# Pair slots for weight parts, and two weight slots lent as staging buffers, in a window-attention and two-MoE-layer kernel

## The chip, the cores and the metric

The kernel runs on one core of one Trainium2 chip. The metric is the device time of one execution in microseconds (us), lower is better. A core has five engines that run side by side, each taking its own instructions in order: TensorE (PE, matmuls), VectorE (DVE), ScalarE (ACT), GpSimd (POOL) and SyncE (SP, used here to issue DMA transfers). They wait for each other by semaphores. PE writes its results into PSUM banks; everything else lies in SBUF.

## The reference

All inputs are float32. Attention with a window of 64 keys over 4 batches, 8 heads, 576 positions and 64 columns a head; then x of 2304 tokens by 512 columns goes through two layers:

```python
scores = scale * np.matmul(q, k.transpose(0, 1, 3, 2))       # window of 64 keys, softmax
x = np.matmul(attn, v)                                       # -> 2304 x 512

h = x @ w_in                                                 # first layer, d_ff 2048
g = np.where(pos, h, np.where(neg, 0.0, (h + beta) ** 2 / (4.0 * beta)))
x = g @ w_out

h = x @ w_in2                                                # second layer, d_ff 1024
solu = h * softmax(h)
ln = (solu - mu) / np.sqrt(var + 1e-06) * g_ln
out = ln @ w_out2
```

## The kernel before

**Numbers in two parts.** A float32 matrix product is made of three products of a faster format: each operand is split into hi and lo, and hi x hi, hi x lo and lo x hi are added. For the first layer the split weights stay in SBUF: for each of 16 ranges f of 128 hidden columns there are `wih{f}`, `wil{f}` (of w_in) and `woh{f}`, `wol{f}` (of w_out), each in a slot of its own in pool `w_p`, named by its tag.

**How a weight comes in.** A *unit* is 128 x 512 float32-pairs of w_in or w_out, 512 KiB. There are 32, in the order w_in range 0, w_out range 0, w_in range 1 and so on; unit n is range n // 2, counted from 0, so "the 15th unit" is unit 14. `w1_unit` picks the slots, `w_unit` takes a staging buffer `st` (tag "st", `NST` = 5 buffers in a ring) and issues the transfer: units 0 to 4 on SP, the others on POOL. Then come three steps, one for each call of `w_conv`: `split_a` (ACT, L132), `split_b` (two DVE instructions, L136 and L137), and `split_c` (ACT writes the hi part, L145; DVE subtracts and writes the lo part, L146). After the L146 of its unit a staging buffer is free. POOL takes its instructions in order too, so a transfer that waits for its buffer holds back all those behind it.

**The stage.** Tokens are worked in six blocks j of 384. For a block and each range f, `moe_h` makes 12 matmuls into `ps_h` (L496, needing wih and wil of f), ACT and DVE turn that into gh and gl (L505, L506, L511, L512, L515), and `moe_y` adds 12 matmuls into four accumulators `acc` (L526, needing woh and wol). Block 0 needs every range's weights for the first time, so it runs along with their arrival; this is the stage that the change touches. The other blocks find all weights in place. After the last block come the products of the second layer (L712) and its output (L827).

**Attention in between.** The blocks' inputs are made between the matmuls: for group g (192 tokens, two heads) PE makes scores `ps_s` (L352), DVE adds the mask and finds the extremum (L360), ACT takes the exponentials (L366), DVE sums and scales (L377 to L386), PE transposes p into `ps_p` (L400, L402), ACT copies that to pT (L405, L407), PE multiplies by v into `ps_x` (L421), and ACT and DVE split the result into xh (L428) and xl (L429). Groups 0 to 7 make block 0's input, 8 to 15 block 1's. Groups 0 to 17 go one by one, later ones in pairs (L442, L476). One group's keys and queries lie in `kq`, in one of two buffers by turns.

**What sets the order.** The program is written as one sequence of such steps, and a scheduler orders each engine's instructions by its own model of when their inputs are there. That includes its model of when a weight transfer lands. On the chip the order of every engine is then fixed.

**Slots lent before.** Queries and keys of the first tokens lie in the slots of ranges 12 to 15 of w_in until those are loaded; the second layer's weights, its sums `xs` and `u` and its split activations later use the slots of both kinds.

Of the kernel before, what the change touches and what calls it, by code (L numbers as in the profile page):

```python
# [20 lines left out]
def kernel(  # L21
# [28 lines left out]
    NG = NTILES * NP  # L50
    NST = 5
    G0, F0, NC, NQ, NV = 6, 2, 4, 6, 7
# [67 lines left out]

    def w_unit(src, hi, lo, gain=None, eng=nc.sync):
        st = stage["p"].tile([128, 512, 2], U32, tag="st", bufs=NST, name="wst")
        if src.shape[0] == 128 and len(src.shape) == 3:
            w_dma = eng.dma_start(out=st.rearrange("p (k f) t -> p k (f t)", k=src.shape[1]), in_=src)  # L124
        else:
            w_dma = eng.dma_start(out=st.rearrange("p f t -> p (f t)"), in_=src)  # L126
        wdma.append(w_dma.ins)
        return st, hi, lo, gain
# [32 lines left out]

    def wtile(tag):
        return w_p.tile([128, 512], F32R, tag=tag, name=tag)

    def w1_unit(f, which):
        if which == 0:
            hi, lo = wtile(f"wih{f}"), wtile(f"wil{f}")
            wih[f] = hi.rearrange("p (k f) -> p k f", k=KC)
            wil[f] = lo.rearrange("p (k f) -> p k f", k=KC)
            src = w_in[:, f * 256:(f + 1) * 256].rearrange("(k p) f -> p k f", p=128)  # L170
        else:
            hi, lo = woh[f], wol[f] = wtile(f"woh{f}"), wtile(f"wol{f}")
            src = w_out[f * 128:(f + 1) * 128, :]
        return w_unit(src, hi, lo, None, nc.sync if len(wdma) < NST else nc.gpsimd)

# [42 lines left out]
    def w2_load(n):  # L218
        hi, lo = w2oh[n], w2ol[n] = wtile(f"woh{n}"), wtile(f"wol{n}")
        for t, z in enumerate((hi, lo)):  # L220
            nc.sync.dma_start(out=as_f32(z), in_=w2d[8 + n][:, t * 512:(t + 1) * 512])
# [23 lines left out]
    def w2_split(n):  # L245
        v_ = w2v.pop(WORDER[n])
        hi, lo = w2h[WORDER[n]], w2l[WORDER[n]] = wtile(f"wih{n}"), wtile(f"wil{n}")
        nc.scalar.copy(hi, v_)
# [12 lines left out]
    def load_qk(g):  # L261
# [3 lines left out]
        if g < NPE:  # L265
            for src, dst, tag, r0, n in (
                (q, qn, "wih", tl * TT, TT // 2),
                (k, kn, "wil", tl * TT - back, (TT + back) // 2),
            ):
                for r in range(2):  # L270
                    if t < 2:
                        a = w_p.tile([128, 512], F32, tag=f"{tag}{14 - 2 * t + r}", name="qkn")
                    else:
                        a = at_p.tile([128, 512], F32, tag="qk", bufs=5, name="qkn")
                    dst[t, r] = a[0:n, :]
            for h0, h1 in ((0, 2), (2, H)) if t == 0 else ((0, H),):
# [391 lines left out]
    def x2_prep(p):  # L668
        r = x2r.pop(p)
        a11, a12, a21, a22 = (r[:, 2 * k:2 * k + 2, 128 * t:128 * t + 128] for t in range(2) for k in range(2))  # L670
        s = [
            (w_p.tile([128, 512], F32, tag=f"{y}{14 + p % 2}", name="xs") if p else
             d_p.tile([128, 512], F32, tag="o", name="xs")).rearrange("p (z k n) -> p z k n", z=2, k=2)
            for y in ("wih", "wil")
        ]
        s1, s2, s3, s4 = (s[z // 2][:, z % 2] for z in range(4))
# [41 lines left out]
    u = {}  # L718
    PARTS = (("P1", "P6", "P7", "P5", "P4"), ("P2", "P3"))

    def st_p(m, y):
# [5 lines left out]
        elif y == "P1":  # L727
            for z in range(4):
                tag = f"{'woh' if z < 2 else 'wol'}{12 + 2 * (z % 2) + p % 2}"
                u[z + 1] = w_p.tile([128, 512], F32, tag=tag, name="u")  # L730
        if y == PARTS[m % 2][0]:
# [69 lines left out]
    def st_t2(m):  # L801
        lnh[m], lnl[m] = {}, {}
        l_ = ln.pop(m)
        for a in range(2):
            hi, lo = wtile(f"woh{8 + 2 * (m % 2) + a}"), wtile(f"wol{8 + 2 * (m % 2) + a}")
            lnh[m][a], lnl[m][a] = (z.rearrange("p (k t) -> p k t", t=128) for z in (hi, lo))
# [188 lines left out]
```

## Time and profile before

| | us |
|---|---|
| median of 3 runs | 706.09 (705.32 to 706.83) |
| profiled execution | 703.17 |
| its span, first to last instruction | 701.4 |
| PE busy in the span | 678.1 (97%) |
| DVE busy | 448.3 (64%) |
| ACT busy | 412.5 (59%) |
| POOL busy | 134.2 (19%) |

The profile is of one execution. Times are counted from the span's start. A row of the time line gives start, length, engine, line, operation and tiles, and in square brackets how long the engine had been idle before it and what ended that. Matmuls overlap, and their ends are modelled: two neighbouring ones are listed with 0.33 us each and start 0.17 us apart. PE is busy nearly everywhere from about 135 us on; its idle time lies in front of that, while weights, attention and the first block go on together.

### The profile page before, as it was taken

Reading aid. Unit: us, or ns where it says so; the run is one execution under the profiler, and the core shown is the slowest. Engines: PE = TensorE matmul, PEld = TensorE weight load, DVE = VectorE, ACT = ScalarE, POOL = GpSimd, SP = SyncE. Lnnn points to the kernel's source line nnn. Section 1 sums busy time; section 2 is a strip of 40 time slices with the busy share of each in tenths; the row PEclk is TensorE's granted clock in tenths of the full one; section 3 lists DMA queues with packets and bytes.
Section 4 is the critical chain, followed back from the end, with each engine's and each line's share of the span. In section 5 each row is a group of like instructions: output and inputs, shape, how many; then the busy total and the mean of one; then the engine's idle time right before and its main releaser. Section 6 shows DMA issues by size and latency. Waiting matters only on the chain.

```text
span 701.4 us, 12574 instructions
## 1 busy us (share of the span) xinstructions
PE 678.1 (97%) x4439; PEld 625.6 (89%) x4439; DVE 448.3 (64%) x1213; ACT 412.5 (59%) x1006; POOL 134.2 (19%) x178
## 2 busy tenths in 40 slices
PE   6899888899999999999999999999999999999998
PEld 5689788799999999999999999999997888888887
DVE  4789889646445555454455552643289999999850
ACT  5889777665656655665566565364455555445451
POOL 1112221100001000021112111662272322220000
PEclk9999999999999999999999999999999999999999
DMA  9996896625353523346351211562024455444331
GB/s 194 253 241 161 218 245 196 148 35 108 72 116 112 116 64 76 77 129 126 85 113 61 106 41 51 173 202 93 1 83 142 155 178 189 158 147 150 103 109 46
DMA packets 150551, 88.94 MB, mean 127 GB/s; under 512 B 118616, under 2 KB 134744, under 8 KB 150488
## 3 DMA queue, kind: packets, MB, share of 16 engines
q1 hardware_dynamic: 135160, 49.84, 30.2%
q0 software_dynamic: 12592, 33.57, 14.9%
q10 hardware_dynamic: 2736, 4.72, 1.8%
q8 instruction: 35, 0.57, 0.3%
q14 instruction: 28, 0.23, 0.1%
HBM read 63.97 MB, written 24.12 MB: 126 GB/s over the span
## 4 chain that ended last, share of the span: by engine, by line
PE 71%; issue 13%; POOL 4%; DVE 4%; DMA 3%; SPq 3%; ACT 2%; POOLq 0%; DVEq 0%
PE acc L526 21%; PE ps_h L496 21%; PE ps_o L827 14%; PE P L712 9%; DMA wst<-in_moe_w_in_dram 3%; POOL wil L249 2%; PE ps_x L476 2%; PE ps_s L442 2%; PE ps_p L402 2%; SPq L279 1%; DVE gl L515 1%; POOL wst L124 1%; SPq L302 1%; POOL wst L126 1%; DVE x2p L692 1%
## 5 line engine op out<-in xcount | busy, mean ns | idle before, releaser
L511 DVE SCALAR_TENSOR_TENSOR u<-u,ps_h 128x384 f32<-128x384 f32 (+1 forms) x98 | 53.3, 544 | 142.3 <-ACT u L506 141.4
L496 PE MATMUL ps_h<-xh,wih 128*128 128x384 f32 (+1 forms) x392 | 132.0, 337 | 3.1 <-ACT wih L145 3.0
L526 PE MATMUL acc<-gl,woh 128*128 128x384 f32 (+1 forms) x392 | 130.3, 334 | 2.1 <-DVE gl L515 2.1
L496 PE MATMUL ps_h<-xl,wih 128*128 128x384 f32 (+1 forms) x392 | 130.7, 334 | 0.4 <-DVE xl L429 0.4
L496 PE MATMUL ps_h<-xh,wil 128*128 128x384 f32 (+1 forms) x392 | 130.9, 334 | 0.0
L526 PE MATMUL acc<-gh,wol 128*128 128x384 f32 (+1 forms) x392 | 129.3, 332 | 0.0
L526 PE MATMUL acc<-gh,woh 128*128 128x384 f32 (+1 forms) x392 | 123.8, 341 | 2.3 <-ACT gh L512 2.3
L505 ACT ACTIVATE u<-ps_h,half 128x384 f32<-128x384 f32 (+1 forms) x98 | 56.1, 574 | 97.5 <-PE ps_h L496 97.3
L515 DVE TENSOR_TENSOR gl<-u,gh 128x384 fp32r<-128x384 f32 (+1 forms) x98 | 62.6, 640 | 35.2 <-ACT gh L512 34.6
L512 ACT CAST gh<-u 128x384 fp32r<-128x384 f32 (+1 forms) x98 | 49.7, 508 | 49.9 <-DVE u L511 34.8
L496 PEld LDWEIGHTS ps_h<-xh,wih 128*128 128x128 f32 x392 | 74.1, 189 | 4.5 <-ACT wih L145 3.6
L526 PEld LDWEIGHTS acc<-gh,woh 128*128 128x128 f32 x392 | 72.0, 188 | 6.2 <-ACT gh L512 3.5
L526 PEld LDWEIGHTS acc<-gl,woh 128*128 128x128 f32 x392 | 73.7, 188 | 3.1 <-DVE gl L515 2.7
L496 PEld LDWEIGHTS ps_h<-xl,wih 128*128 128x128 f32 x392 | 74.1, 189 | 1.0 <-DVE xl L429 0.8
L496 PEld LDWEIGHTS ps_h<-xh,wil 128*128 128x128 f32 x392 | 74.1, 189 | 0.1
L526 PEld LDWEIGHTS acc<-gh,wol 128*128 128x128 f32 x392 | 73.6, 188 | 0.1
L712 PE MATMUL P<-wih,x2p 128*128 128x512 f32 x216 | 71.6, 390 | 0.7 <-DVE x2p L692 0.7
L827 PE MATMUL ps_o<-woh,wol 128*128 128x512 f32 (+1 forms) x152 | 57.6, 379 | 0.0
L827 PE MATMUL ps_o<-woh,woh 128*128 128x512 f32 (+1 forms) x152 | 57.5, 379 | 0.0
L827 PE MATMUL ps_o<-wol,woh 128*128 128x512 f32 (+1 forms) x152 | 57.5, 378 | 0.0
L506 ACT ACTIVATE u<-u 128x384 f32<-128x384 f32 (+1 forms) x98 | 51.1, 522 | 1.9
L712 PEld LDWEIGHTS P<-wih,x2p 128*128 128x128 f32 x216 | 40.4, 188 | 9.2 <-DVE x2p L692 1.1
(123 smaller groups left out, 1191.8 us busy)
## 6 DMA issues: line engine op xcount, KB each, us to landing
wst<-in_moe_w_out_dram POOLq DMA_DIRECT2D x22, 512.0 KB, 7.4
wst<-in_moe_w_in_dram POOLq DMA_DIRECT2D x21, 512.0 KB, 5.5
vw<-in_v_dram SPq DMA_DIRECT2D x32, 256.0 KB, 5.3
lnd<-e SPq DMA_DIRECT2D x16, 512.0 KB, 2.7
lT<-lnd SPq DMA_DIRECT2D x64, 128.0 KB, 3.0
x2d<-xo POOLq DMA_DIRECT2D x24, 192.0 KB, 2.6
out_dram<-o ACTq DMA_DIRECT2D x17, 256.0 KB, 2.0
w2d<-w2st POOLq DMA_DIRECT2D x8, 512.0 KB, 3.0
```

Source lines behind the costliest of these rows:

```text
L249: nc.gpsimd.tensor_tensor(lo, v_, as_f32(hi), op=ALU.subtract)
L402: nc.tensor.transpose(ps[:, i * 128:i * 128 + 128], p[:, i, :], ident)
L442: nc.tensor.matmul(ps[x][64 * c:64 * c + 64, i * 128 + c0:i * 128 + 128], z[r, KQ + i * 64:KQ + i * 64 + 64], z[r, i * 64 + c0:i * 64 + 12 ...
L496: nc.tensor.matmul(ps, a, bb[:, kc, c], start=(n == 0), stop=(n == 3 * KC - 1))
L505: nc.scalar.activation(u, ps, ACTF.Relu, bias=half, scale=0.5)
L506: nc.scalar.activation(u, u, ACTF.Square)
L511: g = nc.vector.scalar_tensor_tensor(u, u, 1.0, ps, op0=ALU.min, op1=ALU.max)
L512: return nc.scalar.copy(hi, u).ins, g.ins
L515: nc.vector.tensor_tensor(lo, u, as_f32(hi), op=ALU.subtract)
L526: nc.tensor.matmul(acc[j, e][:, c], a, bb, start=(f == 0 and n == 0 and c.start == 0), stop=(f == NF - 1 and n == 2),)
L712: nc.tensor.matmul(ps, l, r, start=(n == 0), stop=(n == 5))
L827: nc.tensor.matmul(ps, a[kk // 4][:, kk % 4, :], b[kk][:, c:c + w], start=(n == 0), stop=(n == 3 * NK2 - 1),)
```

## The change

1. The hi and lo part of a weight share one slot of 128 x 2 x 512 (`wi{f}`, `wo{f}`), and all that uses these slots later takes them in pairs.
2. `NX` = 2: from unit 14 on, and up to unit 27, two of each seven units take the slot `wo15` or `wo14` as staging buffer instead of one of the ring's five: units 14 and 21 take wo15, 15 and 22 take wo14. The final contents of these slots are units 31 and 29.
3. Each unit's transfer from unit 6 on is kept behind the one before it in the scheduler's order.

```diff
-    NST = 5
+    NST, NX = 5, 2
...
-    def w_unit(src, hi, lo, gain=None, eng=nc.sync):
-        st = stage["p"].tile([128, 512, 2], U32, tag="st", bufs=NST, name="wst")
+    def w_unit(src, hi, lo, gain=None, eng=nc.sync, slot=None):
+        if slot is None:
+            st = stage["p"].tile([128, 512, 2], U32, tag="st", bufs=NST, name="wst")
+        else:
+            st = w_p.tile([128, 512, 2], U32, tag=slot, name="wst")
...
-    def wtile(tag):
-        return w_p.tile([128, 512], F32R, tag=tag, name=tag)
+    def wpair(tag, dt=F32R):
+        return w_p.tile([128, 2, 512], dt, tag=tag, name=tag)
+
+    def wtiles(tag):
+        t = wpair(tag)
+        return t[:, 0, :], t[:, 1, :]
...
-            hi, lo = wtile(f"wih{f}"), wtile(f"wil{f}")
+            hi, lo = wtiles(f"wi{f}")
...
-            hi, lo = woh[f], wol[f] = wtile(f"woh{f}"), wtile(f"wol{f}")
+            hi, lo = woh[f], wol[f] = wtiles(f"wo{f}")
             src = w_out[f * 128:(f + 1) * 128, :]
-        return w_unit(src, hi, lo, None, nc.sync if len(wdma) < NST else nc.gpsimd)
+        n = len(wdma)
+        x = NX - 1 - (n - 14) % (NST + NX) if n >= 14 else -1
+        slot = f"wo{NF - NX + x}" if x >= 0 and n < 2 * (NF - NX) else None
+        with ExitStack() as order:
+            if n > NST:
+                order.enter_context(tc.issue_after(wdma[-1]))
+            return w_unit(src, hi, lo, None, nc.sync if n < NST else nc.gpsimd, slot)
...
     def x2_prep(p):
...
-        s = [
-            (w_p.tile([128, 512], F32, tag=f"{y}{14 + p % 2}", name="xs") if p else
-             d_p.tile([128, 512], F32, tag="o", name="xs")).rearrange("p (z k n) -> p z k n", z=2, k=2)
-            for y in ("wih", "wil")
-        ]
+        if p:
+            s = wpair(f"wi{14 + p % 2}", F32)
+            s = s[:, 0, :], s[:, 1, :]
+        else:
+            s = [d_p.tile([128, 512], F32, tag="o", name="xs") for _ in range(2)]
+        s = [z.rearrange("p (z k n) -> p z k n", z=2, k=2) for z in s]
...
-            for z in range(4):
-                tag = f"{'woh' if z < 2 else 'wol'}{12 + 2 * (z % 2) + p % 2}"
-                u[z + 1] = w_p.tile([128, 512], F32, tag=tag, name="u")
+            for z in range(2):
+                t = wpair(f"wo{12 + 2 * z + p % 2}", F32)
+                u[z + 1], u[z + 3] = t[:, 0, :], t[:, 1, :]
```

The uses in `w2_load`, `w2_split`, `load_qk` and `st_t2` change in the same way, from two tags to one pair. The order that comes of it differs from about unit 14 to the end of block 0; what follows stands nearly as before.

POOL, the weight transfers of units 13 to 18, with what each waits for: DMASW is the landing of an earlier transfer into the same buffer, DVE the last step of its split. Before:

```order
L126 DMA wst<-in_moe_w_out_dram 128x1024 [waits DMASW3_49,DVE_49]
L124 DMA wst<-in_moe_w_in_dram 128x4x256 [waits DMASW4_49,DVE_49]
L126 DMA wst<-in_moe_w_out_dram 128x1024 [waits DMASW5_49,DVE_49]
L124 DMA wst<-in_moe_w_in_dram 128x4x256 [waits DMASW6_49,DVE_49]
L126 DMA wst<-in_moe_w_out_dram 128x1024 [waits DMASW7_49,DVE_49]
L124 DMA wst<-in_moe_w_in_dram 128x4x256 [waits DMASW0_49,DVE_49]
```

Of the change, the same place:

```order
L129 DMA wst<-in_moe_w_out_dram 128x1024 [waits DMASW3_49,DVE_49]
L127 DMA wst<-in_moe_w_in_dram 128x4x256
L129 DMA wst<-in_moe_w_out_dram 128x1024
L127 DMA wst<-in_moe_w_in_dram 128x4x256 [waits DMASW4_49,DVE_49]
L129 DMA wst<-in_moe_w_out_dram 128x1024 [waits DMASW5_49,DVE_49]
L127 DMA wst<-in_moe_w_in_dram 128x4x256 [waits DMASW6_49,DVE_49]
```

Units 14 and 15 wait for nothing any more, and unit 16 has the wait that unit 14 had.

DVE around the last step of the last split (`wol_1409`, in the change `wo_1373`): p<-p,rs is the scaling of a group's softmax, ISA its first step. Before:

```order
L382 TENSOR_TENSOR p<-p,rs 128x64
L386 TENSOR_TENSOR p<-p,rs 128x256
L146 TENSOR_TENSOR wil_1335<-wst,wih_1334 128x512
L511 SCALAR_TENSOR_TENSOR u<-u,ps_h 128x384
L146 TENSOR_TENSOR wol_1409<-wst,woh_1408 128x512
L515 TENSOR_TENSOR gl<-u,gh 128x384
L360 ISA p,mx<-ps_s,mask 128x64
```

Of the change:

```order
L149 TENSOR_TENSOR wo_1373<-wst,wo_1373 128x512
L392 TENSOR_TENSOR p<-p,rs 128x64
L396 TENSOR_TENSOR p<-p,rs 128x256
L525 TENSOR_TENSOR gl<-u,gh 128x384
L521 SCALAR_TENSOR_TENSOR u<-u,ps_h 128x384
L525 TENSOR_TENSOR gl<-u,gh 128x384
L370 ISA p,mx<-ps_s,mask 128x64
```

The scaling of a group that stood ahead of the last split stands behind it; the ISA that follows is group 15's before and group 14's in the change.

PE at the end of the stage, from the last acc matmuls to the first ones of block 1 (`ps_h`): kq_125 holds groups with odd numbers, kq_124 those with even ones; three instructions make one group's scores or transposes. Before:

```order
L526 MATMUL acc_754<-gl,woh_1408 128x384
L526 MATMUL acc_754<-gh,wol_1409 128x384
L352 MATMUL ps_s<-kq_124 128x128 x3
L421 MATMUL ps_x<-pT,vw 64x64 x6
L402 MATMUL ps_p<-ident,p 128x128 x3
L352 MATMUL ps_s<-kq_125 128x128 x3
L496 MATMUL ps_h<-xh,wih_146 128x384
```

Of the change:

```order
L536 MATMUL acc_735<-gh,wo_1373 128x384
L362 MATMUL ps_s<-kq_125 128x64
L362 MATMUL ps_s<-kq_125 128x128 x2
L431 MATMUL ps_x<-pT,vw 64x64 x6
L410 MATMUL ps_p<-ident,p 64x128
L362 MATMUL ps_s<-kq_124 128x128 x3
L412 MATMUL ps_p<-ident,p 128x128 x2
L431 MATMUL ps_x<-pT,vw 64x64 x6
L412 MATMUL ps_p<-ident,p 128x128 x3
L362 MATMUL ps_s<-kq_125 128x128 x3
L506 MATMUL ps_h<-xh,wi_144 128x384
```

Group 15's scores, ps_x of group 14 and the transposes of group 15 stand ahead of the last acc matmuls before, and behind them in the change.

## Rows read from the trace of the kernel before

**Rows 1.** Stretches: length, busy of PE, PEld, DVE, ACT, POOL, granted clock, DMA share, GB/s.
```profile
57.00:67.20 10.20, 10.20 (x72) 9.81 (x71) 10.14 (x31) 9.22 (x24) 1.42 (x3) 1.00 0.65 171
67.20:121.50 54.30, 48.25 (x310) 44.42 (x309) 48.09 (x131) 41.59 (x99) 11.50 (x18) 1.00 0.89 223
...
129.40:134.32 4.92, 2.57 (x29) 2.18 (x28) 2.95 (x13) 2.32 (x9) 2.12 (x4) 1.00 0.75 182
134.32:701.00 566.68, 561.54 (x3609) 519.56 (x3608) 342.23 (x867) 311.18 (x718) 111.28 (x135) 1.00 0.38 108
```

**Rows 2.** Waits of PE after 134.32 us: us in total, times, longest.
```profile
PE acc L526 <- DVE gl L515: 1.3, 1, 1.3
PE P L712 <- DVE x2p L692: 0.7, 1, 0.7
```

**Rows 3.** Waits of PE in 67.20 to 121.50 us.
```profile
PE ps_h L496 <- ACT wih L145: 3.0, 2, 1.6
PE acc L526 <- ACT gh L512: 2.3, 4, 1.3
PE acc L526 <- DVE gl L515: 0.8, 1, 0.8
```

**Rows 4.** Waits of ACT and of DVE in 67.20 to 121.50 us, the longest.
```profile
ACT wst L132 <- DMA wst<-in_moe_w_in_dram: 7.6, 6, 2.1
...
DVE wst L136 <- DMA wst<-in_moe_w_in_dram: 4.1, 5, 1.2
```

**Rows 5.** Time line of POOL: the issues of units 14, 15, 16, 18 and 31.
```profile
57.84 0.77 POOL L124 DMA_DIRECT2D wst<-in_moe_w_in_dram  x1 [2.13 <-DVE gl L515]
64.20 0.54 POOL L126 DMA_DIRECT2D wst<-in_moe_w_out_dram  x1 [5.60 <-DVE xl L429]
67.09 0.76 POOL L124 DMA_DIRECT2D wst<-in_moe_w_in_dram  x1 [2.35 <-DVE wol L146]
...
73.54 0.76 POOL L124 DMA_DIRECT2D wst<-in_moe_w_in_dram  x1 [5.15 <-DVE wst L137]
...
110.02 0.54 POOL L126 DMA_DIRECT2D wst<-in_moe_w_out_dram  x1 [0.87 <-DVE wil L146]
```

**Rows 6.** The staging tiles wst in 57.00 to 121.50 us: from issue to landing.
```profile
DMA to landing us min/median/max: 4.1/5.3/7.8
```

**Rows 7.** Time line of PE at the end of the stage.
```profile
129.40 0.83 PE L352 MATMUL ps_s<-kq 128*128 128x128 f32 x6
130.16 0.71 PE L421 MATMUL ps_x<-pT,vw 64*64 64x64 f32 x12
133.23 0.52 PE L402 MATMUL ps_p<-ident,p 128*128 128x128 f32 x3 [2.35 <-DVE p L386]
133.58 0.83 PE L352 MATMUL ps_s<-kq 128*128 128x128 f32 x6
134.32 0.44 PE L496 MATMUL ps_h<-xh,wih 128*128 128x384 f32 x1
```

**Rows 8.** Time line of PE around one wait for a weight.
```profile
78.04 0.86 PE L526 MATMUL acc<-gh,woh 128*128 128x384 f32 x4
80.24 0.44 PE L496 MATMUL ps_h<-xh,wih 128*128 128x384 f32 x1 [1.34 <-ACT wih L145]
80.52 0.34 PE L496 MATMUL ps_h<-xl,wih 128*128 128x384 f32 x1
```

**Rows 9.** Time line of ACT: group 15's copies of pT.
```profile
127.51 0.26 ACT L405 COPY pT<-ps_p 64x128 f32<-64x128 f32 x1
127.68 0.36 ACT L407 COPY pT<-ps_p 128x256 f32<-128x256 f32 x1
```

**Rows 10.** Stretches early in the program, columns as in rows 1.
```profile
22.70:26.13 3.43, 3.36 (x38) 3.06 (x38) 1.97 (x14) 2.71 (x13) 0.00 (x0) 1.00 1.07 383
29.54:32.95 3.41, 1.87 (x21) 1.29 (x20) 2.86 (x8) 3.41 (x12) 0.00 (x0) 1.00 1.10 166
32.95:36.36 3.41, 3.41 (x25) 2.97 (x24) 2.54 (x10) 3.38 (x10) 0.54 (x1) 0.50 0.61 98
```

More of the change, by code (lines that the diff above doesn't have):

```diff
@@ L218, in w2_load @@
     def w2_load(n):
-        hi, lo = w2oh[n], w2ol[n] = wtile(f"woh{n}"), wtile(f"wol{n}")
+        hi, lo = w2oh[n], w2ol[n] = wtiles(f"wo{n}")
         for t, z in enumerate((hi, lo)):
@@ L246, in w2_split @@
         v_ = w2v.pop(WORDER[n])
-        hi, lo = w2h[WORDER[n]], w2l[WORDER[n]] = wtile(f"wih{n}"), wtile(f"wil{n}")
+        hi, lo = w2h[WORDER[n]], w2l[WORDER[n]] = wtiles(f"wi{n}")
         nc.scalar.copy(hi, v_)
@@ L265, in load_qk @@
         if g < NPE:
[L266 to L275, printed above, removed]
+            for r in range(2):
+                if t < 2:
+                    a = wpair(f"wi{14 - 2 * t + r}", F32)
+                    a = a[:, 0, :], a[:, 1, :]
+                else:
+                    a = [at_p.tile([128, 512], F32, tag="qk", bufs=5, name="qkn") for _ in range(2)]
+                qn[t, r], kn[t, r] = a[0][0:TT // 2], a[1][0:(TT + back) // 2]
             for h0, h1 in ((0, 2), (2, H)) if t == 0 else ((0, H),):
@@ L670, in x2_prep @@
         a11, a12, a21, a22 = (r[:, 2 * k:2 * k + 2, 128 * t:128 * t + 128] for t in range(2) for k in range(2))
-        s = [
-            (w_p.tile([128, 512], F32, tag=f"{y}{14 + p % 2}", name="xs") if p else
-             d_p.tile([128, 512], F32, tag="o", name="xs")).rearrange("p (z k n) -> p z k n", z=2, k=2)
-            for y in ("wih", "wil")
-        ]
+        if p:
+            s = wpair(f"wi{14 + p % 2}", F32)
+            s = s[:, 0, :], s[:, 1, :]
+        else:
+            s = [d_p.tile([128, 512], F32, tag="o", name="xs") for _ in range(2)]
+        s = [z.rearrange("p (z k n) -> p z k n", z=2, k=2) for z in s]
         s1, s2, s3, s4 = (s[z // 2][:, z % 2] for z in range(4))
@@ L804, in st_t2 @@
         for a in range(2):
-            hi, lo = wtile(f"woh{8 + 2 * (m % 2) + a}"), wtile(f"wol{8 + 2 * (m % 2) + a}")
+            hi, lo = wtiles(f"wo{8 + 2 * (m % 2) + a}")
             lnh[m][a], lnl[m][a] = (z.rearrange("p (k t) -> p k t", t=128) for z in (hi, lo))
```

## The prediction

> **What bounds the kernel now.** I read the table of stretches first. From 134.32 us to the end TensorE (PE) is busy 561.54 of 566.68 us, and PE's list of waits for that part has only 1.3 and 0.7 us [rows 1, 2]; it runs at PE's pace, so what PE gains or loses before 134.32 reaches the end nearly whole. In 57.00 to 67.20 PE is busy all the time. In 67.20 to 121.50 it is busy 48.25 of 54.30 us: 6.05 idle, and its waits there say for what: 3.0 for the first half of a w_in unit (ACT's cast wih), 2.3 for gh, 0.8 for gl [rows 1, 3]. The others have slack as well: DVE 48.09, ACT 41.59 [rows 1]. Nobody is full, so something outside sets the pace. ACT waits 7.6 us and DVE 4.1 for w_in transfers to land, in front of the first steps of a split [rows 4]; both take their instructions in order, so gh and gl queue behind these waits. The POOL rows give the pace: unit 14 is issued at 57.84, unit 31 at 110.02, with 5.60, 2.35 and 5.15 us of waiting before some issues, each ended by DVE [rows 5]. A transfer waits until the last step of the split five units earlier has freed its buffer. That is a loop: issue, landing (4.1 to 7.8 us, median 5.3 [rows 6]), split, issue. 52.18 us for 17 units is 3.07 us a unit, so a turn of one buffer takes about 15.3 us. Last I read the end of the stage, 129.40 to 134.32, where PE waits 2.35 us for DVE [rows 7].
>
> **The change, part by part.** *Pair slots.* Two halves of a weight part lie in one slot. No instruction is added or removed by it; a slot is free when both halves have been read. Neighbouring matmuls read them, one step of 0.17 us apart: four acc matmuls last 0.86, one 0.34, so (0.86 - 0.34) / 3 [rows 8]. I take 0: at most one such step for each of the slots' next writers, ACT and POOL, and those come after 134 us, where only PE has no slack.
>
> *Seven buffers.* Units 14 and 15 have no buffer to wait for; units 16 to 27 wait for the split seven units back. With the same turn of 15.3 us the loop could give a unit each 15.3 / 7 = 2.19 us. The engines need more than that: DVE's 48.09 us lie over 19 units (13 to 31), 2.5 us each. So up to unit 27 the loop stops setting the pace, and DVE and PE do. What can go is PE's 6.05 us and the restart after each wait: four acc matmuls stand from 78.04, the next would start 4 x 0.17 later, at 78.73, and started at 80.24 after 1.34 idle, so 1.51 were lost [rows 8]. Seven such waits [rows 3] at 0.17 more each make 7.2. What stays: units 28 to 31 go back to the ring of five, the two added slots being needed for their own weights by then. Four units at 3.07 instead of 2.5 keep 2.3. I take 7.2 - 2.3 = **4.9 us gained**, between 0 (landings get longer by as much as they start earlier) and 7.2. The sum of work allows it: without waits DVE would pass its last split 54.30 - 48.09 = 6.2 us earlier [rows 1], before the move below.
>
> [...]
>
> *The order moves with it.* The scheduler lays the weights earlier and so leaves attention later. On DVE the scaling of one group's softmax stood ahead of the last split and now stands behind it; on PE the scores of group 15 stood well inside the stage's matmuls and now follow the last of them. Every instruction of that group counts: its scores (129.40 to 130.16, 0.76), ps_x (0.71) and three transposes (133.23 to 133.58, 0.35) are 1.8 us of PE work that leave the stage and land at its end [rows 7]. On POOL no DMA is moved past another; on SP only loads of q and k blocks change places among themselves. At the end PE now takes: scores 15, ps_x 14, transposes 15, scores 16, ps_x 15, transposes 16, scores 17, then the first matmul of the next block. Before: scores 16, ps_x 15, transposes 16, scores 17. Transposes wait for the softmax of their scores: 129.40 to 133.23, 3.83 us [rows 7]. From the last acc matmul to the next block it was 134.32 - 129.40 = 4.92. Now: 3.83 for group 15; 0.12, one of its transposes, until scores 16; 3.83 for group 16; 0.35 and 0.74 for its transposes and scores 17; and 0.3, half of the two copies of pT (0.26 + 0.36 [rows 9]) that ACT has to do among the exponentials of group 16. That is 9.2 us, 4.2 more after rounding, of which 1.8 is the moved work: **2.4 us lost**. Bounds: 2.1 without the copies, 2.7 with both whole. Queued behind the waiting transposes are PE's ps_x 15, from which the last columns of xh for the next block come, and that whole block.
>
> *TensorE's clock.* [...] At the present end of the stage it was busy 2.57 of 4.92, 0.52, and the clock stayed at 1.00 [rows 1]. In the new stretch of 9.2 us PE has 2.57 + 1.8 = 4.4 us of work, 0.48, and for nearly twice as long, so a fall is likely. Its price is 0 if the 3.41 us lie in waits, 1.7 if they are full of matmuls, more if the clock stays down for another such time; I take **0.8 us lost**, half of one, as waits cover half of the stretch. [...]
>
> **Sum.** 4.9 - 2.4 - 0.8 = 1.7 us shorter. The profiled execution took 703.17 us (span 701.4), 2.9 below the median of 706.09; the terms are differences inside one execution, so I take them off the median: 704.4.
>
> **The rivals.** *Clean gain.* The clock holds and nearly all of PE's idle time goes, at units 28 to 31 too: 6.5 - 2.4 = 4.1 shorter, 702.0. For it: in 57.00 to 67.20 DVE was busy 10.14 and PE 10.20 of 10.20 us [rows 1], so both can be full at once. Against it: the thin end.
>
> *Lockstep.* Weights land in time, but DVE, with some 45 us of work left in a shorter stage, and PE wait for each other: only 3.2 of the 7.2 go. 3.2 - 2.4 - 0.8 = 0.0: 706.1, no change to be seen. For it: of PE's 6.1 us of waits 3.1 were for gh and gl, not for weights [rows 3].
>
> *The end eats it (slower).* One mechanism: two softmax chains in a row at a place where PE has nothing else, and behind them the slow clock for the full 1.7 us. It costs 2.4 + 1.7 = 4.1 whatever the stage gives, and decides as soon as the stage gives less than that. With 2.4 given: 1.7 longer, 707.8.
>
> *It does nothing for the transfers.* The DMA engines are full, share 0.89 in the stage [rows 1], so earlier issues land no earlier: 0 gained, 2.4 and 0.8 lost, 709.3. Against it: the stage moves 223 GB/s, and 383 were moved in 22.70 to 26.13 [rows 1, 10].
>
> **How the numbers follow.** A difference under 0.2%, 1.4 us, can't be told from no change here. Forecast 0.40, of which a little over half lies beyond the 0.2%; clean gain 0.22; lockstep 0.20; the end eats it 0.14; nothing for the transfers 0.04. Faster: 0.23 + 0.22 = 0.45. Slower: 0.14 + 0.04 and 0.03 of lockstep = 0.21. Same: the other 0.34. The range leaves out about a tenth on either side: from inside the clean gain, 702.2, to the slower case, 707.8.
>
> **What would show it.** Right: on POOL units 14 and 15 are issued right behind unit 13, near 56 and 57, and unit 18 near 67 (73.54 before [rows 5]); the 11.7 us that ACT and DVE waited for w_in transfers [rows 4] fall to 3 or less and gather at units 28 to 31; PE's idle time before its last acc matmul falls from 6 to about 2 us, and that matmul ends near 123; then come two waits of PE for DVE's p, 2 to 3 us each, and about 9 us pass until the next block's first matmul. Wrong: the last acc matmul still near 127 (the loop was not the limit), only one wait for p at the end (the chains overlap), or a granted clock of 0.50 for longer than 3.41 us.

## The result

The changed kernel takes 710.8 us (median of 6 runs), the kernel before 704.74 (median of 6). The ratio is 1.0082, with a 95% interval of 1.0064 to 1.0100: 6 us slower, where 1.7 us faster were forecast. The profiled execution took 710.39 us, its span is 708.6 us (701.4 before). Line numbers of the changed kernel are 3 higher than before at the split steps (L135 to L149) and 10 higher from L352 on (L362, L506, L536).

The stretches of the changed kernel, columns as in [rows 1]:

```profile
98.15:101.56 3.41, 3.41 (x13) 3.41 (x12) 3.41 (x9) 2.88 (x6) 1.01 (x2) 0.50 0.87 151
128.43:139.59 11.16, 6.61 (x49) 5.31 (x48) 6.56 (x34) 4.71 (x20) 2.72 (x5) 0.67 0.67 170
132.28:139.59 7.31, 4.82 (x29) 3.84 (x28) 3.65 (x19) 2.87 (x12) 1.08 (x2) 0.50 0.86 203
139.59:142.52 2.93, 2.93 (x9) 2.93 (x10) 1.41 (x4) 0.89 (x6) 0.00 (x0) 0.50 1.04 177
```

The last acc matmul starts at 128.26, hardly earlier than before; from the scores right behind it to the next block's first matmul it was 4.92 us [rows 7] and is 11.16; the granted clock is at 0.50 for 3.4 us inside the stage (from 98.15) and for 10.2 us (132.28 to 142.52) around its end. The end of the stage on PE, in the form of [rows 7]:

```profile
128.26 0.34 PE L536 MATMUL acc<-gh,wo 128*128 128x384 f32 x1
128.43 0.83 PE L362 MATMUL ps_s<-kq 128*128 128x64 f32 x6
129.19 0.71 PE L431 MATMUL ps_x<-pT,vw 64*64 64x64 f32 x12
131.96 0.30 PE L410 MATMUL ps_p<-ident,p 128*64 128x128 f32 x1 [2.05 <-DVE p L392]
132.10 1.31 PE L362 MATMUL ps_s<-kq 128*128 128x128 f32 x6
134.48 1.10 PE L431 MATMUL ps_x<-pT,vw 64*64 64x64 f32 x12 [0.64 <-ACT pT L415]
136.62 0.88 PE L412 MATMUL ps_p<-ident,p 128*128 128x128 f32 x3 [1.04 <-DVE p L396]
137.29 1.49 PE L362 MATMUL ps_s<-kq 128*128 128x128 f32 x6
139.59 0.69 PE L506 MATMUL ps_h<-xh,wi 128*128 128x384 f32 x1 [0.81 <-DVE mx L370]
```

Two softmax chains in a row, as forecast, and three things that were not: a wait of 0.64 for pT, longer matmuls at the clock of 0.50 (scores take 1.31 in place of 0.83), and a wait of 0.81 for DVE's mx, the step that reads the last scores out of their PSUM bank. From the code I take it that the block's first `ps_h` waits for that bank; no view names the bank.

What was to get better did not. The waits of ACT and DVE for transfers, and all of PE's, between 67.20 and 117.50 us (the last split ends there), against [rows 3, 4]:

```profile
ACT wst L135 <- DMA wst<-in_moe_w_in_dram: 7.9, 7, 1.4
ACT wst L135 <- DMA wst<-in_moe_w_out_dram: 0.8, 1, 0.8
DVE wst L139 <- DMA wst<-in_moe_w_in_dram: 2.8, 3, 1.7
PE ps_h L506 <- DVE u L521: 2.4, 1, 2.4
PE ps_h L506 <- DVE wi L149: 0.3, 1, 0.3
PE acc L536 <- DVE gl L525: 0.2, 1, 0.2
PE ps_h L506 <- ACT wi L148: 0.2, 1, 0.2
```

The transfers do start earlier, but by less than the buffers allow: unit 18 at 70.22 (73.54 before [rows 5]), unit 31 at 105.14 (110.02); units 14 and 15, whose buffers are free, at 60.17 and 60.93 (57.84 and 64.20). But ACT and DVE wait for w_in as long as ever, 10.7 us against 11.7. PE's one long wait has its cause on DVE. DVE's time line there:

```profile
93.52 0.35 DVE L439 TENSOR_TENSOR xl<-ps_x,xh 128x192 fp32r<-128x192 f32 x1
95.56 0.43 DVE L139 TENSOR_SCALAR wst<-wst 128x512 uint32<-128x512 uint32 x1 [1.69 <-DMA wst<-in_moe_w_in_dram]
95.90 0.68 DVE L149 TENSOR_TENSOR wi<-wst,wi 128x512 fp32r<-128x512 f32 x1
96.50 0.69 DVE L140 SCALAR_TENSOR_TENSOR wst<-wst 128x512 uint32<-128x512 uint32 x1
97.11 0.55 DVE L521 SCALAR_TENSOR_TENSOR u<-u,ps_h 128x384 f32<-128x384 f32 x1
```

A first split step waits 1.69 us for its transfer, two more split steps follow, and u, for which PE stands still from 95.35 to 97.71, comes behind all three. Right after that the clock falls for the first time in the stage (to 0.50, at 98.15).

### The profile page after: what moved, and what is told of

Same layout as the page of the kernel before. It is cut to its first block, busy times and chain, and to the rows that moved or that the text cites. A ratio compares the mean times of both kernels' runs of the same rounds, so it can differ in the third digit from the quotient of the medians.

```text
span 708.6 us, 12557 instructions
## 1 busy us (share of the span) xinstructions
PE 686.1 (97%) x4439; PEld 632.8 (89%) x4439; DVE 448.7 (63%) x1213; ACT 412.0 (58%) x1006; POOL 133.9 (19%) x178
## 3 DMA queue, kind: packets, MB, share of 16 engines
q0 software_dynamic: 12592, 33.57, 14.8%
## 4 chain that ended last, share of the span: by engine, by line
PE 86%; DVE 6%; issue 3%; DMA 2%; ACT 1%; POOL 1%; SPq 1%; DVEq 0%; POOLq 0%
PE ps_h L506 26%; PE acc L536 26%; PE ps_o L838 14%; PE P L723 10%; PE ps_x L486 2%; PE ps_s L362 2%; PE ps_p L412 2%; PE ps_s L452 2%; DMA wst<-in_moe_w_in_dram 1%; PE ps_x L431 1%; DVE gl L525 1%; PE ps_t L344 1%; DMA qk<-in_k_dram 1%; POOL wi L690 1%; DVE wst L139 1%
## 5 line engine op out<-in xcount | busy, mean ns | idle before, releaser
L506 PE MATMUL ps_h<-xh,wi 128*128 128x384 f32 (+1 forms) x784 | 218.2, 340 | 3.7 <-DVE u L521 2.4
L536 PE MATMUL acc<-gh,wo 128*128 128x384 f32 (+1 forms) x784 | 215.6, 337 | 0.1
L506 PEld LDWEIGHTS ps_h<-xh,wi 128*128 128x128 f32 x784 | 145.9, 192 | 5.8 <-DVE u L521 2.7
L536 PEld LDWEIGHTS acc<-gh,wo 128*128 128x128 f32 x784 | 142.5, 188 | 3.4 <-issue 2.6
L506 PE MATMUL ps_h<-xl,wi 128*128 128x384 f32 (+1 forms) x392 | 132.4, 338 | 0.7 <-DVE xl L439 0.7
L536 PE MATMUL acc<-gl,wo 128*128 128x384 f32 (+1 forms) x392 | 130.7, 335 | 1.5 <-DVE gl L525 1.5
L838 PE MATMUL ps_o<-wo,wo 128*128 128x512 f32 (+1 forms) x456 | 102.3, 379 | 0.0
L838 PEld LDWEIGHTS ps_o<-wo,wo 128*128 128x128 f32 x456 | 82.2, 188 | 16.1 <-DVE wo L826 0.2
L723 PE MATMUL P<-wi,x2p 128*128 128x512 f32 x324 | 80.0, 391 | 0.8 <-DVE x2p L703 0.8
L506 PEld LDWEIGHTS ps_h<-xl,wi 128*128 128x128 f32 x392 | 75.4, 192 | 1.3 <-DVE xl L439 1.1
L536 PEld LDWEIGHTS acc<-gl,wo 128*128 128x128 f32 x392 | 73.7, 188 | 2.5 <-DVE gl L525 2.2
L135 ACT ACTIVATE wst<-wst 128x512 f32<-128x512 f32 x48 | 32.9, 685 | 8.8 <-DMA wst<-in_moe_w_in_dram 7.9
```

The costliest lines, as they stand in the source:

```text
L135: nc.scalar.activation(val, val, ACTF.Prelu, scale=2.0 ** -112, alpha=2.0 ** 32)
L506: nc.tensor.matmul(ps, a, bb[:, kc, c], start=(n == 0), stop=(n == 3 * KC - 1))
L536: nc.tensor.matmul(acc[j, e][:, c], a, bb, start=(f == 0 and n == 0 and c.start == 0), stop=(f == NF - 1 and n == 2),)
L723: nc.tensor.matmul(ps, l, r, start=(n == 0), stop=(n == 5))
L838: nc.tensor.matmul(ps, a[kk // 4][:, kk % 4, :], b[kk][:, c:c + w], start=(n == 0), stop=(n == 3 * NK2 - 1),)
```

## Theories

*Order*: what moved with the change costs the time, the buffers themselves do good. *Buffers*: earlier transfers cost it by themselves. *Slots*: pair slots that come free late. *Clock* against *chains*: how much of the end is the half clock, how much the softmax chains. Once the order was found guilty: *attention* (where group 15 stands) against *splits* (where the split steps stand). For the splits in turn *landing* (their transfers have not landed yet) against *queue* (they take the engines' time ahead of u, gh and attention, landed or not).

## Experiments

All times are medians of fresh runs beside runs of the kernel before (its medians: 704.4 to 705.6); ratios are against those.

**Buffers and order taken apart.** The first run has the pair slots without the two lent buffers; every engine then has its instructions in the order of before.

```diff
-    NST, NX = 5, 2
+    NST, NX = 5, 0
```

> The changed kernel without the two added buffers: pair slots and the issue order of the weights stay, five staging buffers in all. Every engine then has its instructions in the order of the kernel before. Theory 'order' (the order that moved with the change costs the time) and theory 'clock' (TensorE's half clock behind the thin end of the stage costs it): the time of the kernel before, 704.7 within 1 us. Theory 'slots' (a pair slot that comes free late costs it): 2 us or more above the kernel before. The early stretch of half clock (33 to 40 us in the changed kernel, 33 to 36 before) shows here whether its length belongs to the change: 3.4 us if pair slots do nothing, 6.8 us if they cause it.

705.54 us, ratio 1.0010 (0.9991 to 1.0030). Pair slots cost nothing that can be told. Its trace also settles the early stretch of half clock, which had made me suspicious, since the changed kernel has 6.83 us of it from 33.29 on and before 3.41 [rows 10]:

```profile
31.72:38.55 6.83, 5.80 (x35) 5.21 (x37) 5.62 (x19) 4.98 (x16) 1.23 (x2) 0.50 0.69 158
```

With the order of before it can be 6.83 as well: its length differs from run to run.

For the next two, every instruction keeps its text and each engine is tied to a recorded order: of before, with seven buffers, and of the change, with five.

```diff
+def keep_order(nc, tc):
+    at = {i.name: i for i in nc.cur_bb.bb.instructions}
+    for text in ORDER.values():
+        row = []
...
+        for one, two in zip(row, row[1:]):
+            tc.add_manual_dep(two, one.name, mybir.DependencyInfo(
+                mybir.DependencyClass.NoSync, mybir.DependencyReason.DATA), reason="order")
```

> The changed kernel with its seven buffers, but each engine is tied to the order of instructions that the kernel before has. Theory 'order': the loss is gone, and what seven buffers give is left, some 700 to 703 against 704.7 of the kernel before; the stage ends with one exposed softmax chain and 4.9 us from the last acc matmul to the next block. Theory 'buffers' (issuing the weights earlier costs the time by itself, by crowded transfers or by full engines): 708 or more, as the changed kernel.

699.98 us, ratio 0.9927 (0.9898 to 0.9955).

> Five buffers, but each engine is tied to the order of instructions that the changed kernel has. Theory 'order': as slow as the changed kernel or slower, 710 to 715, since the weights come as late as before and the end of the stage is the changed one. Theory 'buffers': the time of the kernel before, 704.7 within 1 us.

725.6 us, ratio 1.0283 (1.0252 to 1.0314), 10 us beyond what theory *order* had expected.

| | order of before | order of the change |
|---|---|---|
| five buffers (pair slots) | 705.5 | 725.6 |
| seven buffers | 700.0 | 710.8 |

Buffers are worth 5.5 us in the one order and 14.8 in the other; the order costs 20.1 us with five and 10.8 with seven. So *order* holds and *buffers* falls. With seven buffers in the old order nearly all waits are gone; ACT, DVE's longest, and PE, 67.20 to 117.50 us (the added table moves line numbers by 20):

```profile
ACT wst L155 <- DMA wst<-in_moe_w_in_dram: 0.6, 2, 0.5
ACT wst L155 <- DMA wst<-in_moe_w_out_dram: 0.6, 2, 0.3
...
DVE u L541 <- ACT u L536: 0.2, 1, 0.2
...
PE acc L556 <- ACT gh L542: 0.5, 1, 0.5
PE ps_h L526 <- DVE wi L169: 0.3, 1, 0.3
PE ps_h L526 <- DVE u L541: 0.2, 1, 0.2
```

Its last acc matmul starts at 124.87, and its end is that of [rows 7], one chain:

```profile
128.88 0.52 PE L432 MATMUL ps_p<-ident,p 128*128 128x128 f32 x3 [2.35 <-DVE p L416]
129.23 0.83 PE L382 MATMUL ps_s<-kq 128*128 128x128 f32 x6
129.96 0.44 PE L526 MATMUL ps_h<-xh,wi 128*128 128x384 f32 x1
```

**The clock at the end.** Idle matmuls into columns that nobody reads, with all else in the order of the change; first too many, then fewer.

```diff
+        for _ in range({15: 16, 16: 9}.get(u, 0)):
+            nc.tensor.matmul(ps[:, 384:512], ident, ident, start=True, stop=True)
```

> The changed kernel with 25 idle matmuls of 128x128 at the end of the first stage, 16 ahead of group 15's transposes and 9 ahead of group 16's, into columns that nobody reads; every other instruction keeps its place. They cover PE's waits of 2.05 and 1.04 us for p. Theory 'clock': the granted clock stays at 1.00 there, the 10.2 us at 0.50 are gone, the way from the last acc matmul to the next block falls from 11.2 to about 9 us and the block's first matmuls run at full speed: 3 to 5 us less than the changed kernel's 710.8. Theory 'chains' (the exposed softmax chains cost it, the clock is a bystander): 710.8 within 1 us.

709.77 us, ratio 1.0061 (1.0038 to 1.0085): neither. The clock did hold, but 16 such matmuls last 3.84 us, where PE had waited 2.05; I had reckoned with half of that each, so they delayed what they should have bridged. The fillers of group 15 (each matmul is listed twice), and the clock in two stretches:

```profile
130.02 3.84 PE L428 MATMUL ps_p<-ident 128*128 128x128 f32 x32
128.44:132.28 3.84, 3.74 (x39) 3.41 (x39) 2.90 (x16) 1.84 (x8) 1.64 (x3) 1.00 0.32 107
132.28:140.44 8.16, 6.50 (x64) 5.93 (x62) 3.67 (x19) 2.75 (x12) 1.08 (x2) 1.00 0.86 202
```

```diff
-        for _ in range({15: 16, 16: 9}.get(u, 0)):
+        for _ in range({15: 8, 16: 4}.get(u, 0)):
```

> As the run with 25 idle matmuls at the end of the stage, but with 8 ahead of group 15's transposes and 4 ahead of group 16's: one took 0.23 us there, so these fill 1.8 and 0.9 us, a little less than PE's waits of 2.05 and 1.04, and should delay nothing. Theory 'clock': at a granted clock of 1.00 the way from the last acc matmul to the next block takes some 9.7 us in place of 11.3 and the block behind it 1.3 us less (the run with 25 has shown the latter): 707.8. Theory 'chains': the way stays at 11 us and more, 709.5 or more.

707.49 us, ratio 1.0030 (1.0016 to 1.0044), against 1.0082: 3.3 us below the changed kernel's 710.8. The way from the last acc matmul to the block is 9.8 us at a clock of 1.00, and what follows has it too:

```profile
127.20:136.90 9.70, 7.69 (x75) 6.52 (x73) 6.62 (x34) 4.62 (x21) 2.73 (x5) 1.00 0.57 166
136.90:144.10 7.20, 7.20 (x78) 6.39 (x79) 3.66 (x9) 4.25 (x13) 0.00 (x0) 1.00 0.77 135
```

From the block's first matmul to the end of the span it is 567.6 us (704.5 - 136.88), in the changed kernel 569.0 (708.6 - 139.59). So the half clock cost 1.5 us in the end of the stage and 1.4 behind it; the 4.7 that the way is still longer than before (5.1 from the last acc matmul) is chains and moved work. Both theories hold a part. The rest of the difference between these two traces lies in the stage: the clock does not fall near 98 us here, and the last acc matmul starts 1.2 us earlier (127.05).

**One place at a time.** First, on PE alone, the acc matmuls tied behind the scores of groups 13 to 15:

```diff
+    PIN = {10: 13, 11: 14, 14: 15}
...
-            moe_y(jy, fy, cy)
+            with ExitStack() as order:
+                if jy == 0 and fy in PIN:
+                    order.enter_context(tc.issue_after(s_last[PIN[fy]].ins))
+                moe_y(jy, fy, cy)
```

> The changed kernel with seven buffers and its own schedule, but the acc matmuls of three ranges on PE are tied behind the scores of groups 13, 14 and 15, so that group 15 stands inside the stage again; nothing else is tied. Theory 'end' (the two exposed chains and the half clock behind them are most of the loss): the way from the last acc matmul to the next block falls from 11.3 to about 5 us, 705 or a little less. Theory 'splits' (the weight steps that stand earlier on DVE and ACT are most of it): 709 or more, the waits for transfers of ACT and DVE still some 10 us.

711.9 us, ratio 1.0089 (1.0066 to 1.0112). As theory *splits* said. The way to the next block got 3.4 us shorter (7.9), but the last acc matmul 4.3 later (132.5): 1.8 of it is the work that came back, the rest comes of PE's waits in the stage, 6.5 us in all where the change has 3.1, less the half clock near 98 us, which this trace does not have. Two of them, both for a u behind split steps, and the one chain that is left at the end:

```profile
98.34 0.45 PE L509 MATMUL ps_h<-xh,wi 128*128 128x384 f32 x1 [2.20 <-DVE u L524]
...
116.25 0.41 PE L509 MATMUL ps_h<-xh,wi 128*128 128x384 f32 x1 [1.54 <-DVE u L524]
...
137.86 0.52 PE L415 MATMUL ps_p<-ident,p 128*128 128x128 f32 x3 [3.35 <-DVE p L399]
```

Then the u of the result's section, three places earlier on DVE, all else as in the change:

```diff
 TENSOR_TENSOR xl<-ps_x,xh
+SCALAR_TENSOR_TENSOR u<-u,ps_h
 TENSOR_SCALAR wst<-wst
 TENSOR_TENSOR wi<-wst,wi
 SCALAR_TENSOR_TENSOR wst<-wst
-SCALAR_TENSOR_TENSOR u<-u,ps_h
```

> The changed kernel in its own order on all engines, with one instruction of DVE moved: the u that PE waited 2.36 us for (at 95 us) stands ahead of the split step that waits for its transfer, three places earlier. Theory 'splits' (split steps that wait for transfers hold up u and so PE): that wait and the half clock from 98.15 to 101.56 go, 2.4 + 1.7 us: 706.7. Rival 'moved wait' (the next thing behind the same transfer, gh or the next split, holds PE up instead): 709 or more.

711.32 us, ratio 1.0088 (1.0066 to 1.0109): the rival. PE waits 1.8 us for gh, 1.4 for wi and 1.1 for u in the stage, 4.8 in all where it was 3.1. Mending one wait moves it on. The half clock near 98 us did go in its trace, but around the end it lasts 13.65 us where it was 10.24.

**Splits or attention.** Two complementary halves of the old order, with seven buffers. In the first only the split steps and u, gh, gl are tied among each other, on ACT and DVE, to the end of the stage; in the second attention, the stage's matmuls and u, gh, gl are, on PE, ACT and DVE, and the splits are free. Of the table `ORDER` only those instructions are left.

In words:

```diff
-    ORDER: all instructions of PE, DVE, ACT, POOL, SP
+    ORDER: split_a, split_b, split_c, u, gh, gl on DVE (136) and ACT (126)
```

> The changed kernel with seven buffers; only the split steps of the weights and the steps between the two matmuls (u, gh, gl) are tied to the order of the kernel before among each other, on ACT and DVE, up to the end of the first stage. PE, POOL, SP and all attention steps are free; the schedule then puts group 15 back inside the stage by itself. Theory 'splits' (the loss comes from split steps that stand too early on ACT and DVE and keep attention and u behind waits for transfers): as with the whole old order, 700, ACT waits for transfers 2 us or less in the stage. Theory 'attention' (it matters where the groups stand on each engine, exactly as before): 703 or more.

699.73 us, ratio 0.9922 (0.9899 to 0.9946).

```diff
-    ORDER: all instructions of PE, DVE, ACT, POOL, SP
+    ORDER: attention, xo, ps_h, acc, u, gh, gl on PE (744), DVE (225) and ACT (192)
```

> The counterpart: attention steps and the stage's matmul steps (with u, gh, gl) are tied to the order of the kernel before on PE, ACT and DVE; the split steps are free, and the schedule lays them early, as in the changed kernel. The stage then ends with one exposed chain, 5.1 us. Theory 'splits': the waits of ACT and DVE for transfers stay near 10 us, u and gh stand behind them, PE loses some 4 us in the stage: 704 to 706. Theory 'attention': 700 to 701.

710.13 us, ratio 1.0074 (1.0051 to 1.0096).

The place of the split steps carries the whole loss. With them in their old places among u, gh and gl the scheduler puts group 15 back inside the stage without being told, ACT waits 1.8 us for transfers, and the kernel is as fast as with the whole old order (699.98). With attention in its old places and the splits early, the end is as short as before (5.1 us), and the loss, larger than the 704 to 706 expected, has gone into the stage: its last acc matmul starts at 134.2. PE's waits from 67.20 on to there:

```profile
PE ps_h L526 <- DVE u L541: 3.4, 1, 3.4
PE acc L556 <- ACT gh L542: 1.9, 1, 1.9
PE acc L556 <- DVE gl L545: 0.8, 1, 0.8
PE ps_h L526 <- DVE wi L169: 0.6, 1, 0.6
```

and the stretch with the first of them, at a clock of 0.50:

```profile
94.75:101.58 6.83, 4.91 (x14) 4.40 (x15) 6.31 (x14) 4.33 (x9) 1.31 (x2) 0.50 1.24 247
```

The two long chains at the end are thus a symptom: whichever work is not held in place gives way to the early splits.

**How many buffers.** The old order with six, then with nine:

```diff
-    NST, NX = 5, 2
+    NST, NX = 5, 1
```

> The order of the kernel before on every engine, with six buffers (one added) in place of seven. The loop's arithmetic gives a turn of 15.3 us over six buffers, 2.55 us a unit, and the engines need 2.5: nearly all of what seven gave, 700.5. If the turn gets longer with more transfers on the way, or the gain goes by buffers: about half of it, 702.3.

702.17 us, ratio 0.9954 (0.9936 to 0.9971): 3.0 of the 4.6 us, between the two guesses and nearer to the second. ACT still waits 5.2 us for w_in there.

```diff
-    NST, NX = 5, 2
+    NST, NX = 5, 4
```

> The order of the kernel before on every engine, with nine buffers. With seven PE waited 1.0 us in all in the stage, so at most that is left: 699 to 700. If the loop still set the pace with seven, 2 us or more are gained: 698 or less.

699.63 us, ratio 0.9928 (0.9908 to 0.9949): no more than seven. Seven take what there is.

**Late landing, or engine time?** The same nine in the order of the change:

> The order of the changed kernel on every engine, with nine buffers (four added): units 18 to 27 can be issued earlier, nothing else differs. Theory 'landing' (in the changed order the first split step of a unit stands on ACT and DVE where its transfer has not landed yet): the waits of ACT and DVE for transfers, 8.7 and 3.4 us in the stage, fall to a third for units 20 to 27, PE's wait of 2.4 us at 95 us and the half clock after it go, 706 to 707. Theory 'queue' (the early split steps take DVE's and ACT's time ahead of u, gh and attention, landed or not): 710 or more.

711.93 us, ratio 1.0113 (1.0084 to 1.0142). That looks like theory *queue*, but the run did not do what it was made for: the units were issued no earlier (unit 18 at 69.97, in the changed kernel 70.22). The rows of ACT's first split steps and of POOL's issues in the changed kernel say why:

```profile
85.31 0.72 ACT L135 ACTIVATE wst<-wst 128x512 f32<-128x512 f32 x1 [1.18 <-DMA wst<-in_moe_w_in_dram]
90.11 0.67 ACT L135 ACTIVATE wst<-wst 128x512 f32<-128x512 f32 x1 [1.14 <-DMA wst<-in_moe_w_in_dram]
...
85.62 0.75 POOL L127 DMA_DIRECT2D wst<-in_moe_w_in_dram  x1 [3.80 <-DVE wi L149]
90.43 0.77 POOL L127 DMA_DIRECT2D wst<-in_moe_w_in_dram  x1 [3.52 <-DVE mx L370]
```

ACT starts as a w_in unit lands (22 at 85.31, 24 at 90.11), and 0.3 us later POOL issues the next w_in unit, 24 and 26; the instructions named as its releasers have nothing to do with its buffer. A w_in unit goes out when the one before it has landed: two units in some 5 us, with seven buffers as with nine. The suspect is the room that this kernel's launch sets with `dynamic_dma_scratch_size=1024`; that it bears on POOL's issues is a guess up to the run with 3072. The next three runs have eight buffers: a ring of four and four lent slots, lent from unit 4 on.

```diff
-    NST, NX = 5, 2
+    NST, NX = 4, 4
...
-        x = NX - 1 - (n - 14) % (NST + NX) if n >= 14 else -1
+        x = NX - 1 - (n - 4) % (NST + NX) if n >= 4 else -1
...
```

> The order of the changed kernel on every engine, with eight buffers (a ring of four and four lent slots in turn, lent from the fifth unit on). In every trace so far a w_in unit of POOL's queue was issued 0.33 us behind the landing of the w_in unit before it, wherever its buffer was free: two weight units in about 5.1 us, whatever the number of buffers. If that queue sets the pace, this run is as the changed kernel, 710 to 711. It is the control of the next run.

714.49 us, ratio 1.0143 (1.0123 to 1.0162): worse than the change. Ahead of 57 us PE waits 8.4 us for the first loads of q and k (1.0 with nine buffers lent later, in the order of before); I put that down to the eight early transfers.

```diff
-dynamic_dma_scratch_size=1024
+dynamic_dma_scratch_size=3072
```

> [...] If that room holds the issues back, w_in units are no longer issued 0.33 us behind a landing but as buffers come free, several units earlier. Then theory 'landing' (early split steps lose because their transfers have not landed): the waits of ACT and DVE for transfers fall from some 12 us to 3 or less, PE loses 3 to 4 us less in the stage: 706 to 707. Theory 'queue' (early split steps take the engines' time ahead of u, gh and attention, landed or not): 710 or more though the waits are gone. If the 0.33 us stay, the room is not what holds them.

713.38 us, ratio 1.0118 (1.0101 to 1.0135). The room was it, with nothing else changed: w_in units are now issued ahead of the landing of the one before (unit 20 at 75.17, 3.35 us behind the issue of unit 18, which landed 1.45 later). ACT's wait for w_in in 67.20 to 117.50 us, in the control and with the room:

```profile
ACT wst L155 <- DMA wst<-in_moe_w_in_dram: 7.1, 6, 3.4
```

```profile
ACT wst L155 <- DMA wst<-in_moe_w_in_dram: 3.4, 1, 3.4
```

It fell by half, and the time by 1.1 us, which the two overlapping intervals do not tell from nothing. The end of the stage is unchanged in kind, with PE waiting 2.05, 0.85, 1.04 and 0.81 us. This speaks for late landings as the smaller part, and for early steps that cost mostly by standing ahead of u, gh and the softmax, landed or not. It is not shown, and the shares stay open: the 3.4 us at unit 28 remained, DVE's wait for w_in fell only from 3.0 to 2.0, and both kernels start some 5 us late.

> Eight buffers and the larger room in the order of the kernel before. PE waited 1.0 us in the stage with seven buffers: 699 to 700, within 0.7 us of the seven-buffer run in that order.

710.69 us, ratio 1.0079 (1.0060 to 1.0099), 11 us more than nine buffers in the same order: missed. The start is 5 us late here as well, and the ring of four holds units 28 to 31 back (31 issued at 117.26, with seven buffers at 105.14). This way of lending is a bad one, and only the two eight-buffer runs in the changed order may be read against each other.

**The early clock.** Five idle matmuls ahead of group 6's transposes, where PE waits at 31.4 us; in the seven-buffer kernel with the old order, and in the kernel before.

```diff
+        for _ in range({6: 5}.get(u, 0)):
+            nc.tensor.matmul(ps[:, 384:512], ident, ident, start=True, stop=True)
```

> Seven buffers in the order of the kernel before, and 5 idle matmuls (0.23 us each, 1.15 together) ahead of group 6's transposes, where PE waits 1.37 us at 31.4 us in the kernel before and its clock falls near 33 us in nearly every trace. Theory 'clock': the fall near 33 us goes, 1.7 us for 3.4 us at half speed: 698.3 against 700.0. Rival: the fall comes a little later all the same (the run in the old order had it at 48.8 us), and nothing is won: 700.

698.92 us, ratio 0.9916 (0.9891 to 0.9942); without them 0.9927 (0.9898 to 0.9955): no difference to be told. In its trace the clock fell all the same, to 0.50 at 31.03, for 3.41 us.

> The kernel before with the same 5 idle matmuls in the same place and no other change. Theory 'clock': no granted clock of 0.50 near 33 us, and 1.7 us less than the kernel before (3.4 if its runs often have two such times): 703.3 against 705. Rival: the fall moves to another place, or PE was not the limit there: 705 within 0.7.

703.51 us, ratio 0.9981 (0.9961 to 1.0001): inconclusive. In its trace the clock is 1.00 from 31.00 to 36.40, and 3.41 us at 0.50 from 48.65 take the place of the fall near 33, as the rival said. That trace is of its slowest run, 708.39 us, and has three more such falls, at 82.79, 113.51 and 137.40, where the trace of the kernel before, in the same order but for the five idle matmuls, has none.

## Why the prediction was wrong, point by point

**Pair slots, 0:** right within what can be told (1.0010, 0.9991 to 1.0030).

**Seven buffers, 4.9 us gained:** the right size for the buffers alone, in an order that was not to be had with them: 704.62 - 699.98 = 4.6 us, and the scores behind the last acc matmul start at 125.05 where it was 129.40 [rows 7]. The size came by luck, for the loop was read wrongly. "A transfer waits until the last step of the split five units earlier has freed its buffer" fits two of the five waits in [rows 5], the 2.35 and 0.87 us that end with L146. Unit 18, at 73.54, went out 0.3 us behind the landing of unit 16, which this row of the kernel before gives:

```profile
73.23 0.69 ACT L132 ACTIVATE wst<-wst 128x512 f32<-128x512 f32 x1 [1.57 <-DMA wst<-in_moe_w_in_dram]
```

So did at least four more of the nine w_in units from unit 14 on (issues at 84.61, 90.05, 103.13 and 108.39, ACT's starts on a landing at 84.30, 89.74, 102.82 and 108.08). A free buffer does not help such a unit: the sum had 2.19 us a unit for seven buffers, the changed kernel has 2.53 (units 18 to 26 at 70.22 to 90.43), and that happens to be what DVE needs. In the changed kernel itself the step failed: the waits for w_in stayed at 10.7 us where 3 or less were to be left.

**The order moves with it, 2.4 us lost:** this is the step that failed. It says "The scheduler lays the weights earlier and so leaves attention later" and then prices the second half only, as instructions of group 15 on PE. The first half was the expensive one: split steps moved ahead of u, gh, gl and softmax on ACT and DVE, and no row was asked what an early split step does to those behind it. The rows stood there: ACT's 7.6 and DVE's 4.1 us in front of first split steps [rows 4], with gh and gl queued behind. I took for granted that those waits would end with the loop; but the new order was drawn for transfers that come sooner, and they did not come sooner by as much. The order costs 10.8 us, seen between the seven-buffer runs: the last acc matmul 3.4 us later (128.26 against 124.87), though 1.8 us of group 15's work had left its front; the way to the next block 6.2 longer (11.3 against 5.1); 1.3 behind that. The other traces with seven or nine buffers bear the first of these out: that matmul starts at 127.05 to 128.38 in the order of the change (without the tied acc matmuls) and at 122.98 to 124.87 with the splits in their old places. The 9.2 us foreseen for the stage's end, counted from the scores, were near at full clock (9.65, 127.23 to 136.88 in the run with 12 idle matmuls); DVE's mx, 0.81 us, was not foreseen, and the first chain was shorter than taken (3.52 for 3.83).

**TensorE's clock, 0.8 us lost:** the clock did fall at the end of the stage, but no run shows the 0.8, half of what a fall as long as the one in [rows 10] could cost, an estimate. What the runs showed in its place: 10.2 us at 0.50 around the end cost 1.5 + 1.4, and the 3.4 us at 98.15 another 1.2 to 1.7 (1.7 is half of 3.41, an estimate; between the runs with 25 and with 12 idle matmuls, with this fall and without it, the last acc matmul differs by 1.2: 128.27 and 127.05). The next block's first matmuls ran at 0.50 too (139.59 to 142.52, PE busy all the time). The clock also fell inside the stage, behind a wait of 2.4 us, a place for which the sum had no term.

**Landings:** a unit took 4.3 to 6.2 us from issue to landing in the changed kernel ([rows 6] before), and two more buffers were worth 4.6 to 5.5 us in the order of before.

**Rivals.** "The end eats it" came nearest in what happens: slower, two chains, the slow clock behind them. Its 4.1 us, counted without the 1.8 of moved work, were 5.7 (6.2 - 1.8 + 1.3), and it is not the cause, since the two runs that put group 15 back into the stage gave nothing back. That nothing would be gained on transfers (709.3) came nearest in time, for a wrong reason: in the order of before the same two buffers did gain 4.6 us, so full DMA engines are not what took the gain away; issues were held and the splits came too early.

**Signs named beforehand.** Units 14 and 15 right behind unit 13: no, 60.17 and 60.93 behind 57.49. Unit 18 near 67: 70.22. Waits of 11.7 us to 3 or less: no. PE's idle time in the stage from 6 to about 2: 3.1. Last acc matmul near 123 or, if wrong, near 127: 128.26. Two waits for p of 2 to 3 us: 2.05 and 1.04, of chains that partly overlap with transposes and scores. A clock of 0.50 for longer than 3.41 us: yes, 10.2.

## What to carry over

When a scheduler decides the order, more buffers are two changes: the buffers, and an order drawn for transfers as early as its model has them. Run both halves apart, by tying the engines to the old order, before judging either; here +4.6 us of gain and 10.8 of loss were hidden in one number. Then tie as little as does it: 262 split, u, gh and gl steps on two engines turned 710.8 us into 699.7.

## What the runs showed of the hardware

- POOL's 512 KiB transfers of w_in went out 0.3 us behind the landing of the one before in the order of the change, with seven buffers (85.31 and 85.62, 90.11 and 90.43) and with nine (85.21 and 85.52); so did at least five of nine in the kernel before (73.23 and 73.54). With `dynamic_dma_scratch_size` at 3072 in place of 1024 they went out ahead of it (one at 75.17, by 1.45). The profile names an unrelated instruction as the releaser, or "issue".
- A 128x128 float32 matmul of the filler, back to back, takes 0.24 us (16 in 3.84), not the 0.12 that the list of x32 records suggests: each is listed twice.
- The early fall of the clock comes at 31.03, 31.72, 32.95 and 33.29 us, or not until 48.65, and lasts 3.41 or 6.83 us, with identical orders (3.41 from 32.95 in the kernel before, 6.83 from 31.72 in the run with pair slots alone). Half of the 3.41 between them is 1.7 us; so, by that estimate, a difference of under 2 us between two single traces over that stretch says nothing.
- At the end of the stage too, chance has a part. With one softmax chain of 5.1 to 5.8 us the clock fell to 0.50 for 3.41 us in six traces (pair slots alone at 134.12, six buffers 132.63, splits old 129.12, attention old 139.12, both runs with early idle matmuls 126.61 and 137.40; mean clocks of these traces 0.988 to 0.995) and stayed at 1.00 in four (kernel before; seven, nine and eight buffers in its order; 0.997 to 0.998). With two chains and no idle matmuls it fell for 6.83 to 13.65 us in all six traces (0.979 to 0.990).
